# Transposing Q and K by DMA instead of by TensorE, in a block-sparse attention and MLP-mixer kernel

## The chip, the cores and the metric

The kernel runs on one core of a Trainium2 chip. The metric is device time in microseconds (us), the median of several executions; each experiment was timed against the kernel before on the same chip. A run counts as slow when it is over 1.5% above the fastest of its kernel; slow runs are left out of ratios, and where only a slow run was profiled, the text says so. A profile is one execution taken by the hardware profiler; its span is some 1.7 to 2.1 us shorter than the device time. Engines are called as the profile calls them: PE (TensorE matmul), PEld (its weight load), DVE (VectorE), ACT (ScalarE), POOL (GpSimd) and SP (SyncE, which here only issues DMAs).

## The reference

Four batches, eight heads, 768 positions, head width 64. Attention is masked by 32-wide blocks: neighbours, first and last blocks, and three sampled blocks a row. A token mixer and a channel mixer follow.

```python
scores = scale * np.matmul(q, k.transpose(0, 1, 3, 2))
scores = np.where(mask, scores, -1000000000.0)
attn = softmax(scores)
x = np.matmul(attn, v)                         # per head, then heads side by side: 768 x 512 per batch
h = np.maximum(x.T @ w_tok1, 0.0) @ w_tok2     # token mixing
u = x + h.T
out = u + np.maximum(u @ w_ch1, 0.0) @ w_ch2   # channel mixing
```

## The kernel before

The 32 heads go in 16 pairs. Each pair's K and Q arrive as bf16 with positions on partitions; the score matmul is given them with the 64 head columns on partitions. 24 further partitions (64 to 87) of the same tiles hold block indicators and mask rows, so one 88-row matmul gives the masked score.

```python
raw = sbw.tile([128, 2, NC, D], BF16, tag=f"{nm}raw", bufs=NR, ...)   # NR = 4; loaded by POOL, fp32 -> bf16
...
lay = sbw.tile([128, NC, 2, D], BF16, tag=f"{nm}lay", bufs=2, ...)
nc.vector.tensor_copy(out=lay, in_=raw.rearrange("p h c d -> p c h d"))
...
for c in range(NC):                                     # NC = 6, on PE, into PSUM
    nc.tensor.matmul(out=box["t"][:, c, :], lhsT=lays[nm][:, c, :, :], rhs=ident, is_transpose=True)
for hd in range(2):                                     # evacuated by DVE or ACT
    nc.vector.tensor_copy(out=buf[0:64, :], in_=box["t"][64 * hd : 64 * hd + 64, :, :])
...
nc.tensor.matmul(out=ps[:, hd, 0:384], lhsT=ktb[n][0:88, 128 * j : 128 * j + 128],
                 rhs=qtb[n][0:88, 384 * half : 384 * half + 384], start=True, stop=True)
nc.scalar.activation(out=et, in_=ps[:, :, 0:384], func=AF.Exp, scale=0.125)      # 192 of these
```

The order of instructions is made at build time. A small planner simulates PE, ACT and DVE with estimated durations and emits whatever is ready first, by priority: scores, then PV (attention times V), transposes, token mixing, and last channel mixing, which fills what PE time is left. In the traces each engine runs its list **in order**, and an instruction waits for its data whatever the planned durations are.

The softmax here doesn't subtract the row's maximum and nothing guards it: scores larger than these inputs give would overflow.

Of the kernel before, what the change touches and what calls it, by code (L numbers as in the profile page):

```python
# [8 lines left out]
FP32 = mybir.dt.float32  # L9
BF16 = mybir.dt.bfloat16  # L10
# [40 lines left out]
class Planner:  # L51
# [11 lines left out]
    def __init__(self, slots):  # L63
        self.now = 0.0
        self.free_at = {"pe": 0.0, "act": 0.0, "dve": 0.0}
        self.streams = []
        self.ops = []
        self.count = 0
        self.slots = {tag: [Ev(0.0)] * n for tag, n in slots.items()}
        self.exp_pending = 0  # L70
# [32 lines left out]
    def step(self):  # L103
# [3 lines left out]
        if self.free_at["pe"] <= self.now:  # L107
            for s in self.streams:
# [4 lines left out]
                cost, deps, tags, emit, done = s[3]  # L113
# [15 lines left out]
        else:  # L129
            nxt.append(self.free_at["pe"])  # L130
        for eng in ("act", "dve"):
            if self.free_at[eng] > self.now:
# [37 lines left out]
def kernel(  # L170
# [21 lines left out]
    NR = 4  # L192
    NET = 8

    sb1 = ctx.enter_context(tc.tile_pool(name="sb1", bufs=1))
# [12 lines left out]
    vaug = [sb1.tile([128, 2, NC, 66], BF16, name=f"vaug{n}") for n in range(NV)]  # L208
    qtb = [sb1.tile([128, S], BF16, name=f"qtb{n}") for n in range(2 * NV)]
    ktb = [sb1.tile([128, S], BF16, name=f"ktb{n}") for n in range(2 * NV)]  # L210

    P = Planner({"ps": 2, "po": 1, "pm": 3, "et": NET, "a_t": 2, "o": 3, "rc": 2,
                 "lay": 2, "kq": NV, "va": NV})
    US = 1e3
# [110 lines left out]

    rows_there = {("k", n): Ev() for n in range(2 * NV)} | {("q", n): Ev() for n in range(2 * NV)}

    def mask_stream():
# [15 lines left out]
        for h in range(2):  # L344
            def copy(eng, h=h):
                nc.scalar.copy(out=qtb[0][R, 384 * h : 384 * h + 384], in_=pms[h][R, 0:384])
            e2.append(P.op(("act",), {"act": 420.0}, [done], copy, prio=0))
            rels[h].same_as = e2[h]
        rows_there["q", 0].same_as = e2[1]
        for n in range(2 * NV):  # L350
            for nm, bufs in (("k", ktb), ("q", qtb)):
                if (nm, n) == ("q", 0):
                    continue

                def copy(eng, n=n, nm=nm, bufs=bufs):
                    nc.vector.tensor_copy(
                        out=bufs[n][R, :], in_=indf if nm == "k" else qtb[0][R, :]
                    )
                rows_there[nm, n].same_as = P.op(
                    ("dve",), {"dve": 300.0}, e2, copy, prio=2 if n < 2 else 6  # L360
                )
# [4 lines left out]

    ones_there = [Ev() for _ in range(NV)]

    START = 6.5 * US
# [13 lines left out]
    def relayout(p):  # L383
        lays = {}
        for nm in ("k", "q", "v"):
            raw = raws.pop((nm, p))
            arr = arrive.pop((nm, p))

            def emit(eng, nm=nm, raw=raw):
                if nm == "v":  # L390
                    nc.vector.tensor_copy(out=vaug[p % NV][:, :, :, 0:64], in_=raw[:, :, :, :])  # L391
                    return
                lay = sbw.tile([128, NC, 2, D], BF16, tag=f"{nm}lay", bufs=2, name=f"{nm}lay{p}")
                nc.vector.tensor_copy(  # L394
                    out=lay[:, :, :, :], in_=raw[:, :, :, :].rearrange("p h c d -> p c h d")
                )
                lays[nm] = lay

            deps = [arr]
            if nm == "v" and p >= NV:  # L400
                deps.append(pv_done[p - NV])
            if nm != "v" and p >= 2:
                deps.append(qT_there[p - 2, 1])
            lays[nm + "ev"] = P.op(("dve",), {"dve": 320.0}, deps, emit, prio=2 if nm != "v" else 3)
            copied[nm, p] = lays[nm + "ev"]
        va_there[p] = lays["vev"]
        return lays

    def transposes(p):
        for hd in range(2):  # L410
            kT_there[p, hd], qT_there[p, hd] = Ev(), Ev()
        yield lambda: ("v", p) in raws
        lays = relayout(p)
        for nm, bufs, there in (("k", ktb, kT_there), ("q", qtb, qT_there)):
            box, last, rel = {}, Ev(), Ev()
            for c in range(NC):
                def emit(nm=nm, c=c, box=box, rel=rel):
# [7 lines left out]
                    )  # L425
                deps = [lays[nm + "ev"]]
                if p >= NV:
                    deps.append(qk_done[p - NV])
                yield 56.0, deps, [("pm", 1)] if c == 0 else [], emit, last if c == NC - 1 else None
            n_left = [2]  # L430
            for hd in range(2):
                buf = bufs[2 * (p % NV) + hd]

                def evac(eng, hd=hd, buf=buf, box=box):
                    i = box["t"][64 * hd : 64 * hd + 64, :, :].rearrange("p c s -> p (c s)")
                    if eng == "act":
                        nc.scalar.copy(out=buf[0:64, :], in_=i)
                    else:
                        nc.vector.tensor_copy(out=buf[0:64, :], in_=i)  # L439

# [5 lines left out]
    def alias(a, b):  # L446
        a.same_as = b
# [9 lines left out]
    def qk_stream():  # L457
        for s in steps:
# [4 lines left out]
            def emit(s=s, done=done, rel=rel):  # L463
# [4 lines left out]
                for hd in range(2):  # L468
                    n = 2 * (p % NV) + hd
                    nc.tensor.matmul(  # L470
                        out=ps[:, hd, 0:384], lhsT=ktb[n][0:88, 128 * j : 128 * j + 128],
                        rhs=qtb[n][0:88, 384 * half : 384 * half + 384], start=True, stop=True,
                    )
                P.exp_pending += 1

                def exp(eng):
# [12 lines left out]
                326.0,  # L489
                [e for hd in range(2) for e in (  # L490
                    kT_there[p, hd], qT_there[p, hd],
                    rows_there["k", 2 * (p % NV) + hd], rows_there["q", 2 * (p % NV) + hd],
                )],
# [74 lines left out]
    def tok(b, g):  # L568
# [16 lines left out]
        if b not in st:  # L585
            st[b] = dict(u=xs[b], uT_there=[Ev() for _ in range(4)])
        a_rel = Ev()
# [33 lines left out]
        for dmc in (2 * g, 2 * g + 1):  # L621
            last, rel, tbox = Ev(), Ev(), {}
            for sc in range(NC):
                def emit(sc=sc, dmc=dmc, rel=rel, tbox=tbox):
                    if sc == 0:
                        P.take("pm", rel)
                        tbox["pt"] = psM.tile([128, NC, 128], BF16, tag="pm", name=f"pm_ut_{b}_{dmc}")
# [3 lines left out]
                    )  # L631
                yield 56.0, [u_evs[sc // 2]], [("pm", 1)] if sc == 0 else [], emit, last if sc == NC - 1 else None

            def evac(eng, dmc=dmc, tbox=tbox):
                if "uT" not in st[b]:
                    st[b]["uT"] = sbw.tile([128, 4, S], BF16, tag="uT", bufs=B, name=f"uT{b}")
                o, i = st[b]["uT"][:, dmc, :], tbox["pt"][:, :, :].rearrange("p c s -> p (c s)")
# [9 lines left out]
    def ch(b, pool, tag):  # L647
# [4 lines left out]
        for cc in range(12):  # L652
            for sh in range(2):
# [23 lines left out]
                alias(rel, ev)  # L677
                rc_there[cc, sh] = ev
        for sc in range(NC):
            last, rel, pbox = Ev(), Ev(), {}  # L680
# [51 lines left out]
    P.stream(4, ch_stream())  # L732
    P.stream(-1, mask_stream())
    tok2_op = P.op(("dve",), {"dve": 900.0}, [tok2_raw], wtok2_lay, prio=3)

# [56 lines left out]
```

## Time and profile before

| | before |
|---|---|
| device time | 288.56 us (288.53 to 288.65) |
| PE busy | 269.9 us, 94% |
| last exp ends (attention over) | 160.9 us |
| channel matmuls before that | 44 |
| longest gap between exps | 3.0 us, at 32 us |
| DMA engines full until | about 62 us |

The page gives each engine's busy time and then the span in 40 slices, one digit each. The lines that carry the argument are in the prediction below. The last exp's end comes from the ACT timeline.

### The profile page before, as it was taken

The numbers are of one execution on the slowest core, as the hardware profiler recorded it, in microseconds if no ns is written. First come the engines' busy times: TensorE is split into PE (matmuls) and PEld (weight loads), VectorE is DVE, ScalarE is ACT, GpSimd is POOL, SyncE is SP. The second block draws the span as 40 slices with busy tenths as digits, with TensorE's granted clock in tenths as the row PEclk, the third lists the DMA queues.
The fourth block names the chain that finished last, engine by engine and source line by source line (L and its number), as shares of the span: only waits on it lengthen the run. The fifth ranks groups of instructions, "written<-read, shape, count | busy, mean of one in ns | idle before, by whom it ended". The sixth has DMA issues, their size and how long they took to land.

```text
span 287.1 us, 6351 instructions
## 1 busy us (share of the span) xinstructions
PE 269.9 (94%) x2682; PEld 175.5 (61%) x2690; DVE 130.2 (45%) x286; ACT 191.9 (67%) x286; POOL 45.0 (16%) x70
## 2 busy tenths in 40 slices
PE   0799899999999999999999999999999999999994
PEld 0366676678777777777777754456544654456441
DVE  5789966557777569765546341210022001200121
ACT  1589999999999999999999642037501770067200
POOL 7956554522211000000000000000000000000000
PEclk9999999999999999999999999999999999999999
DMA  4999999996254100000000001220022001210122
GB/s 55 134 204 202 214 201 205 201 185 87 39 73 66 23 2 2 0 2 3 2 0 2 2 0 39 106 76 0 2 110 84 29 0 73 94 54 0 38 102 82
DMA packets 19168, 20.07 MB, mean 70 GB/s; under 512 B 1348, under 2 KB 15428, under 8 KB 19140
## 3 DMA queue, kind: packets, MB, share of 16 engines
q0 software_dynamic: 15648, 13.37, 30.3%
q1 hardware_dynamic: 3492, 6.29, 5.8%
q8 instruction: 21, 0.34, 0.5%
q14 instruction: 7, 0.06, 0.1%
HBM read 26.74 MB, written 6.29 MB: 115 GB/s over the span
## 4 chain that ended last, share of the span: by engine, by line
PE 73%; ACT 14%; DVE 6%; issue 2%; DMA 2%; POOL 2%; POOLq 0%; DVEq 0%; ACTq 0%
PE pm_ch L686 22%; PE pm_ch L664 21%; ACT et L478 14%; PE ps L470 14%; PE po L520 8%; PE pm_tok L578 3%; PE pm_tok L603 2%; DMA kraw<-in_k_dram 2%; DVE qtb L439 1%; PE pm_ut L628 1%; PE tq L421 1%; DVE ktb L439 1%; PE tk L421 1%; DVE x L535 1%; DVE klay L394 1%
## 5 line engine op out<-in xcount | busy, mean ns | idle before, releaser
L478 ACT ACTIVATE et<-ps 128x768 bf16<-128x768 f32 x192 | 143.2, 810 | 4.2 <-PE ps L470 3.2
L470 PE MATMUL ps<-qtb,ktb 88*128 88x384 bf16 x384 | 95.3, 329 | 4.0 <-ACT et L478 1.7
L560 ACT ACTIVATE rc<-pm_ch 128x384 bf16<-128x384 f32 x84 | 41.2, 491 | 60.7 <-PE pm_ch L664 44.8
L520 PEld LDWEIGHTS <-et 128*128 128x128 bf16 x1152 | 56.0, 97 | 22.8 <-DVE x L535 1.9
L664 PE MATMUL pm_ch<-uT,w_ch 128*128 128x384 bf16 x384 | 68.6, 326 | 0.2 <-DVE rc L562 0.2
L686 PE MATMUL pm_ch<-w_ch,rc 128*128 128x512 bf16 x280 | 62.4, 379 | 0.4
L520 PE MATMUL po<-vaug,et 128*128 128x65 bf16 x1152 | 61.5, 193 | 0.5 <-ACT et L478 0.2
L694 DVE TENSOR_TENSOR o<-pm_ch,x 128x512 f32<-128x512 f32 x24 | 16.6, 692 | 98.7 <-PE pm_ch L686 98.7
L664 PEld LDWEIGHTS <-w_ch 128*128 128x128 bf16 x384 | 37.0, 98 | 23.1 <-issue 0.3
L686 PEld LDWEIGHTS <-rc 128*128 128x128 bf16 x288 | 28.2, 98 | 33.6
L470 PEld LDWEIGHTS <-ktb 88*128 88x128 bf16 x384 | 34.2, 99 | 11.9 <-issue 4.4
L439 DVE COPY ktb<-tk 64x768 bf16<-64x768 bf16 x29 | 16.0, 552 | 17.5 <-PE tk L421 17.2
L611 DVE TENSOR_TENSOR x<-pm_tok,x 128x512 bf16<-128x512 f32 x24 | 16.2, 687 | 6.8 <-PE pm_tok L603 6.5
L535 DVE TENSOR_TENSOR x<-po,recip 128x384 bf16<-128x384 f32 x32 | 17.8, 557 | 1.1
L439 DVE COPY qtb<-tq 64x768 bf16<-64x768 bf16 x30 | 16.6, 552 | 2.1 <-PE tq L421 1.1
L603 PE MATMUL pm_tok<-a_t,w_tok 128*128 128x256 bf16 x96 | 17.0, 272 | 0.0
L230 POOL DMA_DIRECT2D vraw<-in_v_dram x16 | 12.3, 766 | 28.4 <-DVE vaug L391 25.7
L578 PE MATMUL pm_tok<-x,w_tok 128*128 128x256 bf16 x96 | 16.3, 272 | 0.0
L230 POOL DMA_DIRECT2D kraw<-in_k_dram x16 | 11.6, 727 | 7.7 <-DVE recip L534 2.2
L230 POOL DMA_DIRECT2D qraw<-in_q_dram x16 | 11.5, 720 | 6.4 <-DMA w_ch<-in_moe_w_ch_dram 2.4
L534 DVE RECIPROCAL recip<-po 128x6 f32<-128x6 f32 x32 | 6.2, 195 | 12.0 <-PE po L520 11.6
L421 PE MATMUL tq<-ident,qlay 128*128 128x128 bf16 x96 | 11.3, 230 | 0.2 <-DVE qlay L394 0.2
(49 smaller groups left out, 122.8 us busy)
## 6 DMA issues: line engine op xcount, KB each, us to landing
out_dram<-o SPq DMA_DIRECT2D x24, 256.0 KB, 2.0
kraw<-in_k_dram POOLq DMA_DIRECT2D x16, 192.0 KB, 7.9
qraw<-in_q_dram POOLq DMA_DIRECT2D x16, 192.0 KB, 7.4
vraw<-in_v_dram POOLq DMA_DIRECT2D x16, 192.0 KB, 7.0
w_ch<-in_moe_w_ch_dram POOLq DMA_DIRECT2D x8, 384.0 KB, 9.8
w_tok<-in_moe_w_tok_dram POOLq DMA_DIRECT2D x1, 384.0 KB, 7.8
w_tok2r<-in_moe_w_tok_dram POOLq DMA_DIRECT2D x1, 384.0 KB, 9.0
samp<-in_sampled_blocks_dram SPq DMA_DIRECT2D x1, 0.6 KB
```

Source lines behind the costliest of these rows:

```text
L230: nc.gpsimd.dma_start(out=raw[:, :, :, :], in_=APx(src, 2 * p * S * D, [[NC * D, 128], [S * D, 2], [1, NC * D]]),)
L421: nc.tensor.matmul(out=box["t"][:, c, :], lhsT=lays[nm][:, c, :, :].rearrange("p h d -> p (h d)"), rhs=ident[:, :], start=(c == 0), stop=( ...
L439: nc.vector.tensor_copy(out=buf[0:64, :], in_=i)
L470: nc.tensor.matmul(out=ps[:, hd, 0:384], lhsT=ktb[n][0:88, 128 * j : 128 * j + 128], rhs=qtb[n][0:88, 384 * half : 384 * half + 384], star ...
L478: nc.scalar.activation(out=et[:, :, :], in_=ps[:, :, 0:384], func=AF.Exp, scale=0.125)
L520: nc.tensor.matmul(out=po[:, hd, c, :], lhsT=et[:, hd, 128 * c : 128 * c + 128], rhs=va[:, hd, j, 0:65], start=(j == 0 and hd == 0 and c = ...
L535: nc.vector.tensor_tensor(out=free(xs[b][:, 3 * half, 128 * pb : 128 * pb + 128], 0, [[64, 2], [DM, 3], [1, 64]]), in0=po[:, :, :, 0:64], ...
L560: nc.scalar.activation(out=o(), in_=i, func=AF.Relu)
L578: nc.tensor.matmul(out=box["pm"][:, t, :], lhsT=w_tok1[:, sc, 128 * t : 128 * t + 128], rhs=xs[b][:, sc, 256 * g : 256 * g + 256], start=( ...
L603: nc.tensor.matmul(out=ubox["pm"][:, i, :], lhsT=w_tok2[:, t, 2 * s2 + i, :], rhs=a_t[:, t, :], start=(i == 0 and t == 0), stop=(i == 1 an ...
L664: nc.tensor.matmul(out=pbox["pm"][:, 0:384], lhsT=w_ch1[:, dmc, 128 * cc : 128 * cc + 128], rhs=st[b]["uT"][:, dmc, 384 * sh : 384 * sh + ...
L686: nc.tensor.matmul(out=pbox["pm"][:, :], lhsT=box["rc"][:, cc, 128 * sc : 128 * sc + 128], rhs=w_ch2[:, cc, :], start=(cc == 0), stop=(cc ...
```

## The change

The aim is to take the transposes off PE, and their evacuations off DVE and ACT. From the third pair on, DVE copies raw K and Q into a *wide* tile of 128 columns per head: 64 data columns and 24 mask columns, which were put there once. A DMA transpose (`dma_start_transpose`, in the code and below called the crossbar) writes the whole wide tile, transposed, straight into the operand of the score matmul. These pairs need no PSUM tile and no evacuation: 12 transposes of K and 12 of Q are left on PE, of 96 each. The queue of SP issues the transfers, two for each pair, 393 KB each.

```diff
+    NPE = 2          # pairs 0 and 1 stay with PE
+    NL = 3           # wide buffers for each of K and Q
-    qtb = [sb1.tile([128, S], BF16, name=f"qtb{n}") for n in range(2 * NV)]
+    qtb = [sb1.tile([128, 2, S], BF16, name=f"qtb{n}") for n in range(NV)]
+    wide = {(nm, n): sb1.tile([128, 2, NC, 128], BF16, name=f"{nm}wide{n}")
+            for n in range(NL) for nm in ("k", "q")}
...  # wide_stream: 12 small matmuls, 6 clears and 6 copies put the mask columns into the wide tiles, once
+                elif p >= NPE:
+                    nc.vector.tensor_copy(out=wide[nm, p % NL][:, :, :, 0:64], in_=raw[:, :, :, :])
...
+    def crossbar(p):
+        lays = relayout(p)
+        for nm, bufs, there in (("k", ktb, kT_there), ("q", qtb, qT_there)):
+            def emit(eng, nm=nm, bufs=bufs):
+                nc.sync.dma_start_transpose(
+                    out=bufs[p % NV][:, :, :].rearrange("e h (c s) -> e (h c) s", c=NC),
+                    in_=wide[nm, p % NL][:, :, :, :].rearrange("p h c e -> p (h c e)"),
+                )
...
+            ev = P.op(("sp",), {"sp": 1500.0}, deps, emit, prio=1, lat=2500.0)   # planned: 1.5 + 2.5 us
+            xb_done[nm, p] = ev
+            there[p, 0], there[p, 1] = ev, ev
...
-                    st[b]["uT"] = sbw.tile([128, 4, S], BF16, tag="uT", bufs=B, name=f"uT{b}")
+                            st[b]["uT"] = sbw.tile([128, 4, S], BF16, tag="uT", bufs=3, name=f"uT{b}")
```

More of the change, by code (lines that the diff above doesn't have):

```diff
@@ L64, in __init__ @@
         self.now = 0.0
-        self.free_at = {"pe": 0.0, "act": 0.0, "dve": 0.0}
+        self.free_at = {"pe": 0.0, "act": 0.0, "dve": 0.0, "sp": 0.0}
         self.streams = []
@@ L130, in step @@
             nxt.append(self.free_at["pe"])
-        for eng in ("act", "dve"):
+        for eng in ("act", "dve", "sp"):
             if self.free_at[eng] > self.now:
@@ L208 @@
     vaug = [sb1.tile([128, 2, NC, 66], BF16, name=f"vaug{n}") for n in range(NV)]
-    qtb = [sb1.tile([128, S], BF16, name=f"qtb{n}") for n in range(2 * NV)]
-    ktb = [sb1.tile([128, S], BF16, name=f"ktb{n}") for n in range(2 * NV)]
+    qtb = [sb1.tile([128, 2, S], BF16, name=f"qtb{n}") for n in range(NV)]
+    ktb = [sb1.tile([128, 2, S], BF16, name=f"ktb{n}") for n in range(NV)]
+    wide = {
+        (nm, n): sb1.tile([128, 2, NC, 128], BF16, name=f"{nm}wide{n}")
+        for n in range(NL) for nm in ("k", "q")
+    }
     P = Planner({"ps": 2, "po": 1, "pm": 3, "et": NET, "a_t": 2, "o": 3, "rc": 2,
-                 "lay": 2, "kq": NV, "va": NV})
+                 "uT": 3})
     US = 1e3
@@ L324 @@
     indf = ind[R, :, :].rearrange("k c p -> k (c p)")
-    rows_there = {("k", n): Ev() for n in range(2 * NV)} | {("q", n): Ev() for n in range(2 * NV)}
+    rows_there = {(nm, n): Ev() for nm in ("k", "q") for n in range(2 * NPE)}
+    wide_there = {(nm, n): Ev() for nm in ("k", "q") for n in range(NL)}
     def mask_stream():
@@ L345, in copy @@
             def copy(eng, h=h):
-                nc.scalar.copy(out=qtb[0][R, 384 * h : 384 * h + 384], in_=pms[h][R, 0:384])
+                nc.scalar.copy(
+                    out=qtb[0][R, 0, 384 * h : 384 * h + 384], in_=pms[h][R, 0:384]
+                )
             e2.append(P.op(("act",), {"act": 420.0}, [done], copy, prio=0))
@@ L349, in mask_stream @@
         rows_there["q", 0].same_as = e2[1]
-        for n in range(2 * NV):
+        for n in range(2 * NPE):
             for nm, bufs in (("k", ktb), ("q", qtb)):
@@ L356, in copy @@
                     nc.vector.tensor_copy(
-                        out=bufs[n][R, :], in_=indf if nm == "k" else qtb[0][R, :]
+                        out=bufs[n // 2][R, n % 2, :], in_=indf if nm == "k" else qtb[0][R, 0, :]
                     )
@@ L367, with wide_stream, emit, clear @@
     ones_there = [Ev() for _ in range(NV)]
+    def wide_stream():
+        box, done, rel = {}, Ev(), Ev()
+        def emit():
+            P.take("pm", rel)
+            box["m"] = psM.tile([128, 2, NC, 24], FP32, tag="pm", name="pm_wide")
+            for i, rhs in enumerate((ident[R, 64:88], t2add[R, :])):
+                for c in range(NC):
+                    nc.tensor.matmul(
+                        out=box["m"][:, i, c, :], lhsT=ind[R, c, :], rhs=rhs,
+                        start=(i == 0 and c == 0), stop=(i == 1 and c == NC - 1),
+                    )
+        yield 500.0, [Ev(12.5 * US)], [("pm", 1)], emit, done
+        for n in range(NL):
+            for i, nm in enumerate(("k", "q")):
+                def clear(eng, nm=nm, n=n):
+                    nc.vector.memset(wide[nm, n][:, :, :, 64:128], 0.0)
+                def copy(eng, nm=nm, n=n, i=i):
+                    nc.vector.tensor_copy(
+                        out=wide[nm, n][:, :, :, 64:88],
+                        in_=free(box["m"][:, i, 0, :], 0, [[0, 2], [24, NC], [1, 24]]),
+                    )
+                ev = P.op(("dve",), {"dve": 420.0}, [], clear, prio=6)
+                ev = P.op(("dve",), {"dve": 450.0}, [done, ev], copy, prio=6)
+                wide_there[nm, n].same_as = ev
+                rel.same_as = ev
     START = 6.5 * US
@@ L391, in emit @@
                     nc.vector.tensor_copy(out=vaug[p % NV][:, :, :, 0:64], in_=raw[:, :, :, :])
-                    return
-                lay = sbw.tile([128, NC, 2, D], BF16, tag=f"{nm}lay", bufs=2, name=f"{nm}lay{p}")
-                nc.vector.tensor_copy(
-                    out=lay[:, :, :, :], in_=raw[:, :, :, :].rearrange("p h c d -> p c h d")
-                )
-                lays[nm] = lay
+                elif p >= NPE:
+                    nc.vector.tensor_copy(out=wide[nm, p % NL][:, :, :, 0:64], in_=raw[:, :, :, :])
+                else:
+                    lay = sbw.tile([128, NC, 2, D], BF16, tag=f"{nm}lay", bufs=1, name=f"{nm}lay{p}")
+                    nc.vector.tensor_copy(
+                        out=lay[:, :, :, :], in_=raw[:, :, :, :].rearrange("p h c d -> p c h d")
+                    )
+                    lays[nm] = lay
             deps = [arr]
@@ L401, in relayout @@
                 deps.append(pv_done[p - NV])
-            if nm != "v" and p >= 2:
-                deps.append(qT_there[p - 2, 1])
+            if nm != "v" and 1 <= p < NPE:
+                deps.append(qT_there[p - 1, 1])
+            if nm != "v" and p >= NPE:
+                deps.append(wide_there[nm, p % NL])
+                if p - NL >= NPE:
+                    deps.append(xb_done[nm, p - NL])
             lays[nm + "ev"] = P.op(("dve",), {"dve": 320.0}, deps, emit, prio=2 if nm != "v" else 3)
@@ L407, in relayout @@
         return lays
+    xb_done = {}
+    def crossbar(p):
[5 more added lines that the diff above has]
+                    in_=wide[nm, p % NL][:, :, :, :].rearrange("p h c e -> p (h c e)"),
+                )
+            deps = [lays[nm + "ev"]]
+            if p >= NV:
+                deps.append(qk_done[p - NV])
+            ev = P.op(("sp",), {"sp": 1500.0}, deps, emit, prio=1, lat=2500.0)
+            xb_done[nm, p] = ev
+            there[p, 0], there[p, 1] = ev, ev
     def transposes(p):
+        yield lambda: ("v", p) in raws
+        if p >= NPE:
+            crossbar(p)
+            return
         for hd in range(2):
             kT_there[p, hd], qT_there[p, hd] = Ev(), Ev()
-        yield lambda: ("v", p) in raws
         lays = relayout(p)
@@ L425, in emit, with evac @@
                     )
-                deps = [lays[nm + "ev"]]
-                if p >= NV:
-                    deps.append(qk_done[p - NV])
-                yield 56.0, deps, [("pm", 1)] if c == 0 else [], emit, last if c == NC - 1 else None
-            n_left = [2]
+                yield 56.0, [lays[nm + "ev"]], [("pm", 1)] if c == 0 else [], emit, last if c == NC - 1 else None
             for hd in range(2):
-                buf = bufs[2 * (p % NV) + hd]
-                def evac(eng, hd=hd, buf=buf, box=box):
+                def evac(eng, hd=hd, buf=bufs[p % NV], box=box):
                     i = box["t"][64 * hd : 64 * hd + 64, :, :].rearrange("p c s -> p (c s)")
                     if eng == "act":
-                        nc.scalar.copy(out=buf[0:64, :], in_=i)
+                        nc.scalar.copy(out=buf[0:64, hd, :], in_=i)
                     else:
-                        nc.vector.tensor_copy(out=buf[0:64, :], in_=i)
+                        nc.vector.tensor_copy(out=buf[0:64, hd, :], in_=i)
                 ev = P.op(("dve", "act"), {"dve": 550.0, "act": 740.0}, [last], evac, prio=2)
@@ L468, in emit @@
                 for hd in range(2):
-                    n = 2 * (p % NV) + hd
+                    n = p % NV
                     nc.tensor.matmul(
-                        out=ps[:, hd, 0:384], lhsT=ktb[n][0:88, 128 * j : 128 * j + 128],
-                        rhs=qtb[n][0:88, 384 * half : 384 * half + 384], start=True, stop=True,
+                        out=ps[:, hd, 0:384], lhsT=ktb[n][0:88, hd, 128 * j : 128 * j + 128],
+                        rhs=qtb[n][0:88, hd, 384 * half : 384 * half + 384],
+                        start=True, stop=True,
                     )
@@ L489, in qk_stream @@
                 326.0,
-                [e for hd in range(2) for e in (
-                    kT_there[p, hd], qT_there[p, hd],
-                    rows_there["k", 2 * (p % NV) + hd], rows_there["q", 2 * (p % NV) + hd],
+                [e for hd in range(2) for e in [kT_there[p, hd], qT_there[p, hd]] + (
+                    [rows_there["k", 2 * p + hd], rows_there["q", 2 * p + hd]] if p < NPE else []
                 )],
@@ L585, in tok @@
         if b not in st:
-            st[b] = dict(u=xs[b], uT_there=[Ev() for _ in range(4)])
+            st[b] = dict(u=xs[b], uT_there=[Ev() for _ in range(4)], uT_rel=Ev())
         a_rel = Ev()
@@ L625, in emit @@
                     if sc == 0:
+                        if dmc == 0:
+                            P.take("uT", st[b]["uT_rel"])
+                            st[b]["uT"] = sbw.tile([128, 4, S], BF16, tag="uT", bufs=3, name=f"uT{b}")
                         P.take("pm", rel)
@@ L631, in emit @@
                     )
-                yield 56.0, [u_evs[sc // 2]], [("pm", 1)] if sc == 0 else [], emit, last if sc == NC - 1 else None
+                tags = [("pm", 1)] if sc == 0 else []
+                if sc == 0 and dmc == 0:
+                    tags.append(("uT", 1))
+                yield 56.0, [u_evs[sc // 2]], tags, emit, last if sc == NC - 1 else None
             def evac(eng, dmc=dmc, tbox=tbox):
-                if "uT" not in st[b]:
-                    st[b]["uT"] = sbw.tile([128, 4, S], BF16, tag="uT", bufs=B, name=f"uT{b}")
                 o, i = st[b]["uT"][:, dmc, :], tbox["pt"][:, :, :].rearrange("p c s -> p (c s)")
@@ L678, in ch @@
                 rc_there[cc, sh] = ev
+        alias(st[b]["uT_rel"], last)
         for sc in range(NC):
@@ L733 @@
     P.stream(-1, mask_stream())
+    P.stream(-1, wide_stream())
     tok2_op = P.op(("dve",), {"dve": 900.0}, [tok2_raw], wtok2_lay, prio=3)
```

## The prediction

> **What bounds the kernel now.** I read the busy table and the row of slices first. Columns: engine, busy time, share of the span, instructions; then one digit per fortieth of the span (7.2 us).
>
> ```profile
> PE 269.9 (94%) x2682; PEld 175.5 (61%) x2690; DVE 130.2 (45%) x286; ACT 191.9 (67%) x286; POOL 45.0 (16%) x70
> ...
> PE   0799899999999999999999999999999999999994
> ...
> ACT  1589999999999999999999642037501770067200
> ...
> DMA  4999999996254100000000001220022001210122
> ```
>
> TensorE is full from about slice 7 to the end. ScalarE is full in the first 22 slices (to about 161 us): attention, 192 exps. After that only the channel MLP is left. The DMA engines are full until about 62 us (the loads run ahead of need) and nearly idle afterwards.
>
> A busy PE is not yet a PE that cannot take more, so I counted its work by spacing between starts. The chain of waits, ordered by time, gives the spacings (start, length, what, count):
>
> ```profile
> 144.07 0.39 PE pm_ut L628 x7
> ...
> 189.61 15.60 PE pm_ch L664 x96
> ...
> 205.48 10.74 PE pm_ch L686 x49
> ```
>
> A 128x128 transpose every 56 ns (0.39/7), a 384-column matmul every 162.5 ns, a 512-column one every 219 ns. By the same scaling a 65-column PV matmul takes about 29 ns (groups of 6 stand 0.18 us apart), a 256-column one 109 ns. The busy table by stretch (length, then busy and count of PE, PEld, DVE, ACT, POOL, then clock and DMA):
>
> ```profile
> 12.00:36.00 24.00, 21.86 (x267) 15.18 (x266) 22.26 (x54) 21.29 (x29) 14.40 (x20) 1.00 1.20 201
> 36.00:60.00 24.00, 23.08 (x321) 17.05 (x320) 13.58 (x33) 23.90 (x33) 13.09 (x18) 1.00 1.28 202
> 60.00:161.00 101.00, 100.70 (x1419) 76.98 (x1418) 66.33 (x144) 100.33 (x135) 7.16 (x10) 1.00 0.21 30
> 161.00:288.00 127.00, 121.09 (x664) 64.49 (x670) 20.82 (x32) 42.64 (x86) 0.00 (x0) 0.99 0.13 50
> ```
>
> With counts per source line: in 60 to 161 us PE does 271 QK x 163 = 44.2, 814 PV x 29.3 = 23.9, 133 token matmuls x 109 = 14.5, 72 output transposes x 56 = 4.0, 96 Q/K transposes x 56 = 5.4 and 44 channel matmuls = 7.2: 99.2 of 101 us. So **from 60 us on, PE really is full**: what attention leaves free is filled with channel work of batch 0. In 36 to 60 us the same sum is 21.4 of 24, and in 12 to 36 us about 18 of 24: there the fill does not exist yet, because batch 0 has not been through attention (channel matmuls: 2 before 60 us). The early part is set by ACT and DVE. ACT, as a timeline:
>
> ```profile
> 16.88 15.16 ACT L478 ACTIVATE et<-ps 128x768 bf16<-128x768 f32 x20 [0.16 <-PE ps L470]
> 31.96 1.61 ACT L437 COPY ktb<-tk 64x768 bf16<-64x768 bf16 x2
> 33.91 0.80 ACT L437 COPY qtb<-tq 64x768 bf16<-64x768 bf16 x1 [0.33 <-DVE qtb L439]
> 34.99 27.51 ACT L478 ACTIVATE et<-ps 128x768 bf16<-128x768 f32 x37 [0.29 <-PE ps L470]
> ```
>
> Exps come every 27.51/37 = 0.743 us, except for one hole of 3.0 us (31.96 to 34.99), in which ACT evacuates Q/K transposes because DVE (22.26 of 24 busy) is behind.
>
> [...]
>
> **The change part by part.**
>
> 1. Removed from PE: 14 pairs x 2 x 6 = 168 transposes x 56 ns = 9.4 us. Per-stretch counts of the transposes: 72 before 36 us, 24 in 36 to 60, 96 after 60. Minus 24 that stay (pairs 0 and 1), 72 removed ones lie before 60 us, where PE has holes, and save nothing directly. The **96 after 60 us save 96 x 56 = 5.4 us** on the bounding engine, since channel work moves into the freed time.
> 2. Removed from DVE and ACT: 56 evacuations of 64x768, at 552 ns on DVE (59 there in all) or 795 on ACT (5). About 28 us of DVE and 2.4 us of ACT go. The ACT hole at 32 us should vanish; of its 3.0 us I count **2 us**, since batch 0 then finishes attention earlier and the full stretch of PE begins earlier.
> 3. Added to PE: 12 matmuls of 24 columns for the padded tiles[...].
> 4. Added to DVE: 6 clears of 128x768 and 6 PSUM copies of 288 elements. From the rows for 512 (692 ns) and 384 elements (551 ns), a copy of 288 is about 445 ns; a clear I put at 400 to 700 ns (a 24x768 memset took 698). Together 5 to 7 us. Against it 15 - 7 = 8 mask-row copies x 0.36 = 2.9 us go. The relayout copies (370 ns) stay as copies into the wide tiles. In 12 to 36 us DVE should come out lighter: four pairs of evacuations (4 x 4 x 0.55 = 8.8 us) leave.
> 5. Added to SP and DMA: 28 crossbar transposes of 128x1536 bf16, 393 KB each (twice the useful bytes, because of the padding), 11 MB against the 20 MB moved now. No output store leaves before 177 us, so SP is free for them.
> 6. The buffers of uT go from 4 to 3: token work of batch 3 waits until channel-1 of batch 0 is through. That is 96 x 162.5 = 15.6 us of fill, which before did half of by 161 us (46 matmuls) and the changed kernel about 7.2 + 5.4 = 12.6 us or more. The wait falls in the last token group, where other channel work can stand in: about 0.
>
> Sum if the crossbar keeps up: 5.4 + 2 - 0.6 = 6.8 us, 288.56 - 6.8 = 281.8 us, 2.3% less; with the whole hole won and all of ACT's early losses, some 279; with no early gain 283.5.
>
> **Rivals.**
>
> (a) **The crossbar becomes the bound.** Pair 2's exps begin at about 32 us (24 exps done at 16.88 + 15.16), pair p's at 32 + 8.92 (p - 2), since a pair is 12 x 0.743 = 8.92 us; pair 15's at 148. Pair 2's K is laid out at 17.5 us now, so the first transfer can start at about 20. The 28 transfers have 128 us, less some 2 us for landing (output stores land in 2.0): 4.5 us each is the most that hides. [...]5 or 6 us is not excluded, and each microsecond over 4.5 costs about 28 us at the end of attention, of which PE's channel work hides little, because the order on PE is fixed at build time (the schedule assumes 1.5 us plus 2.5 latency). At 6 us: about 288 + 30 = 320.
>
> (b) **Contention early.** Until 62 us the loads keep the DMA engines full. The first four to eight transposes share them and may take twice as long; pair 2 has 12 us for two, pair 3 has 21 for four. For it: the 1.2 in the DMA column. Against it: the loads run 8 pairs ahead and can give way. Cost if it bites: one to five microseconds of ACT and PE standing still near 32 us, so 283 to 287: within 2%.
>
> (c) **Hidden anyway.** If PE had slack after 60 us, nothing would come of the transposes. The count of 99.2 of 101 speaks against it. If only ACT bound (the chain shows ACT alone from 99 to 126 us), attention would still end at about 158 to 161, and the gain would appear as channel matmuls done before then; it is in the sum.
>
> **How range and chances follow.** I give the crossbar two chances in three to keep up. Then 279 to 284, faster by over 2% (below 282.8) in some 63%: 0.42. Contention or a smaller early gain leaves it within 2% (282.8 to 294.3): 0.25. Crossbar slower than about 4.7 us: 0.33. The middle of all this is a little above the clean sum: 282.5. The range leaves a tenth above 306, for a crossbar well over 5 us.
>
> **What would show it.** Right: no ACT copies after the second pair, exps at 0.743 us without a hole near 32 us, attention ending at 157 to 161 us with 75 or more channel matmuls before it (46 now), PE full to the end, transposes landing within about 4 us. Wrong: PE waiting at the QK matmuls for a DMA into ktb or qtb, exps spaced by transfers and not by 0.743, SP's queue never empty, DMA busy through 150 us; or early DVE time going up with the clears, with pair 2 late. I am most wrong if one 128x1536 transpose takes over 4.5 us.

The sum came to 5.4 + 2 - 0.6 = 6.8 us, so 288.56 - 6.8 = 281.8 us; in the changed kernel the twelve keep PE busy for 0.49 us.

## The result, and the profile after

The changed kernel takes **316.37 us** (median of 4, 315.43 to 317.63), against 288.54 for the kernel before in the same rounds. The ratio is 1.097, with a 95% interval of 1.092 to 1.102. Here and below a ratio is the mean time of one kernel's fast runs over the mean of the other's of the same rounds, so it is not quite the ratio of the medians quoted. The prediction (about 282.5, with a range that ends at 306) was wrong.

The busy table and the slices of the changed kernel (one digit per fortieth of the span, here 7.84 us):

```profile
PE 265.4 (85%) x2525; PEld 169.6 (54%) x2534; DVE 109.4 (35%) x247; ACT 185.6 (59%) x273; POOL 44.9 (14%) x70
...
PE   0798200059999999999999999999999999999995
...
ACT  1589100029999999999999999212750274027400
...
PEclk9999755558999999999999999999999999999999
DMA  3999999999999999555550000022002200220022
```

There is one hole, in slices 5 to 9, in which PE and ACT do nothing, while the DMA row stays at 9. PEclk, the clock granted to PE in tenths, falls to 5 there. The ACT timeline puts the hole between 32.65 and 67.20 us (in brackets, what ended the idle time):

```profile
67.20 1.51 ACT L539 ACTIVATE et<-ps 128x768 bf16<-128x768 f32 x2 [34.55 <-PE ps L530]
...
72.55 123.47 ACT L539 ACTIVATE et<-ps 128x768 bf16<-128x768 f32 x164 [0.58 <-PE ps L530]
```

From 72.55 us on the kernel is as full as before, and an exp takes 123.47/164 = 0.753 us, as before (132 in 99.22 us, 0.752). The queue of SP, as a timeline (start, length, line, what), shows what happened there:

```profile
24.02 7.93 SPq L461 DMA_TRANSPOSE ktb<-kwide  x1
32.01 11.07 SPq L461 DMA_TRANSPOSE qtb<-qwide  x1
43.13 17.23 SPq L461 DMA_TRANSPOSE ktb<-kwide  x2
60.41 5.47 SPq L461 DMA_TRANSPOSE qtb<-qwide  x2
...
158.91 1.43 SPq L461 DMA_TRANSPOSE ktb<-kwide  x1
160.44 1.75 SPq L461 DMA_TRANSPOSE qtb<-qwide  x1
```

The same instruction takes 1.4 to 1.9 us late in the kernel and 8 to 11 us at the start. This length is how long the instruction holds SP's queue, not how long the data move: for the last two transposes the busy table by stretch shows the DMA engines at work from 160.1 to about 163.85 us, 786 KB in 3.75 us, some 210 GB/s or 1.9 us for each. As a sign that the DMA engines are held up it serves all the same, and below it is called the time on SP. From issue to landing, late transposes take 3.8 to 4.2 us; the first two, K and Q, took 20.3 and 21.2. The order of issue shows a second thing: the first two are K and Q of pair **3**. Pair 2 comes third (K) and fifth (Q), because pair p uses wide buffer p mod 3 and buffer 2 got its mask columns last. DVE and PE, as timelines (what ended the idle time is in brackets):

```profile
63.50 0.36 DVE L432 COPY kwide<-kraw 128x768 bf16<-128x768 bf16 x1 [33.64 <-DMA ktb<-kwide]
...
64.00 0.56 DVE L595 TENSOR_TENSOR x<-po,recip 128x384 bf16<-128x384 f32 x1
```

```profile
64.61 0.37 PE L638 MATMUL pm_tok<-x,w_tok 128*128 128x256 bf16 x1 [31.22 <-DVE x L595]
66.31 1.44 PE L530 MATMUL ps<-qtb,ktb 88*128 88x384 bf16 x4 [1.33 <-DMA qtb<-qwide]
```

DVE stood 33.6 us at a copy into a wide buffer that the crossbar had still to read. A norm of pair 1 stood behind that copy, and a token matmul on PE behind the norm. Then PE waited 1.3 us more for Q of pair 2 itself. So two things end within 3 us of each other: DVE's stand at 63.5, and the arrival of Q at 66.3.

The sum in parts. The last exp ends at 196.0 us instead of 160.9, 35.1 later. Of these, 31.6 are the hole (34.6 in place of 3.0), 0.6 its later start, and 2.9 come after it. Most of the 2.9 lie before 72.55 us, where four exps take 5.35 us and the granted clock (the column before the last two) is still 0.51:

```profile
66.30:72.55 6.25, 6.24 (x39) 3.87 (x40) 1.02 (x2) 3.13 (x4) 1.43 (x2) 0.51 1.31 180
```

From the last exp to the end of the span the kernel needs 117.6 us instead of 126.2, 8.6 less: 96 channel matmuls are done before the last exp instead of 44, and 52 x 162.5 ns is 8.5 us. This is the gain that was meant; why it is more than the 5.4 us predicted was not separated. 35.1 less 8.6 is 26.5 us, the difference of the spans (313.6 and 287.1).

### The profile page after: what moved, and what is told of

Its sections match the earlier page's. It is cut to its first block, busy times and chain, and to the rows that moved or that the text cites. A ratio compares the mean times of both kernels' runs of the same rounds, so it can differ in the third digit from the quotient of the medians.

```text
span 313.6 us, 6075 instructions
## 1 busy us (share of the span) xinstructions
PE 265.4 (85%) x2525; PEld 169.6 (54%) x2534; DVE 109.4 (35%) x247; ACT 185.6 (59%) x273; POOL 44.9 (14%) x70
## 3 DMA queue, kind: packets, MB, share of 16 engines
q0 software_dynamic: 15648, 13.37, 28.7%
q1 hardware_dynamic: 47396, 17.31, 27.6%
HBM read 26.74 MB, written 6.29 MB: 105 GB/s over the span
## 4 chain that ended last, share of the span: by engine, by line
PE 78%; DMA 7%; ACT 5%; SPq 4%; DVE 2%; issue 1%; POOL 1%; POOLq 0%; ACTq 0%
PE pm_ch L728 20%; PE pm_ch L751 19%; PE ps L530 19%; PE po L580 10%; DMA ktb<-kwide 6%; ACT et L539 5%; SPq L461 4%; PE pm_tok L638 3%; PE pm_tok L663 3%; DMA qtb<-qwide 2%; PE pm_ut L691 2%; PE tk L487 0%; DVE o L759 0%; DVE eq L320 0%; POOL kraw L236 0%
## 5 line engine op out<-in xcount | busy, mean ns | idle before, releaser
L539 ACT ACTIVATE et<-ps 128x768 bf16<-128x768 f32 x192 | 143.8, 809 | 41.3 <-PE ps L530 40.6
L530 PE MATMUL ps<-qtb,ktb 88*128 88x384 bf16 x384 | 98.3, 339 | 5.0 <-ACT qtb L497 1.6
L728 PE MATMUL pm_ch<-uT,w_ch 128*128 128x384 bf16 x384 | 72.3, 326 | 0.0
L580 PEld LDWEIGHTS <-et 128*128 128x128 bf16 x1152 | 57.7, 99 | 23.6 <-issue 2.7
L620 ACT ACTIVATE rc<-pm_ch 128x384 bf16<-128x384 f32 x73 | 35.8, 491 | 54.9 <-PE pm_ch L728 39.0
L751 PE MATMUL pm_ch<-w_ch,rc 128*128 128x512 bf16 x279 | 62.8, 379 | 0.6 <-DVE o L759 0.2
L580 PE MATMUL po<-vaug,et 128*128 128x65 bf16 x1152 | 62.7, 195 | 0.4 <-ACT et L539 0.3
L530 PEld LDWEIGHTS <-ktb 88*128 88x128 bf16 x384 | 36.1, 100 | 49.3 <-issue 38.7
L759 DVE TENSOR_TENSOR o<-pm_ch,x 128x512 f32<-128x512 f32 x24 | 16.6, 691 | 89.7 <-PE pm_ch L751 89.7
L638 PE MATMUL pm_tok<-x,w_tok 128*128 128x256 bf16 x96 | 17.1, 285 | 31.2 <-DVE x L595 31.2
L432 DVE COPY kwide<-kraw 128x768 bf16<-128x768 bf16 x14 | 5.2, 379 | 35.4 <-DMA ktb<-kwide 35.3
L236 POOL DMA_DIRECT2D vraw<-in_v_dram x16 | 11.5, 721 | 40.3 <-DVE vaug L430 30.3
L622 DVE TENSOR_SCALAR rc<-pm_ch 128x384 bf16<-128x384 f32 x23 | 12.7, 554 | 11.2 <-PE pm_ch L728 11.1
L705 DVE COPY uT<-pm_ut 128x768 bf16<-128x768 bf16 x14 | 7.8, 557 | 4.9 <-PE pm_ut L691 4.9
```

Of the source, the lines that this page charges most:

```text
L236: nc.gpsimd.dma_start(out=raw[:, :, :, :], in_=APx(src, 2 * p * S * D, [[NC * D, 128], [S * D, 2], [1, NC * D]]),)
L530: nc.tensor.matmul(out=ps[:, hd, 0:384], lhsT=ktb[n][0:88, hd, 128 * j : 128 * j + 128], rhs=qtb[n][0:88, hd, 384 * half : 384 * half + 38 ...
L539: nc.scalar.activation(out=et[:, :, :], in_=ps[:, :, 0:384], func=AF.Exp, scale=0.125)
L580: nc.tensor.matmul(out=po[:, hd, c, :], lhsT=et[:, hd, 128 * c : 128 * c + 128], rhs=va[:, hd, j, 0:65], start=(j == 0 and hd == 0 and c = ...
L620: nc.scalar.activation(out=o(), in_=i, func=AF.Relu)
L638: nc.tensor.matmul(out=box["pm"][:, t, :], lhsT=w_tok1[:, sc, 128 * t : 128 * t + 128], rhs=xs[b][:, sc, 256 * g : 256 * g + 256], start=( ...
```

## The experiments

**The theory:** the loads, which fill the DMA engines until about 60 us, slow the transposes that run beside them. The rivals: the first transposes are slow of themselves; or the static order (pair 3 before pair 2, DVE's copy ahead of the norm) makes the hole.

### e1: the same order, few bytes loaded

```diff
+            if p < NR:    # full load; from pair 4 on only 16 of 384 elements a row
-                in_=APx(src, 2 * p * S * D, [[NC * D, 128], [S * D, 2], [1, NC * D]]),
+                in_=APx(src, 2 * p * S * D, [[NC * D, 128], [S * D, 2], [1, 16]]),
...  # w_ch1, w_ch2: memset by POOL instead of loaded; raw tiles kept, so that all is initialised
```

> Same instruction order as the changed kernel, but the loads of pairs 4 to 15 move 16 elements a row instead of 384 and the channel weights are set by memset (wrong result on purpose). Theory (the loads slow the first transposes): the first six transposes take at most 2.5 us each on the SP queue instead of 8 to 11, land within 6 us, ScalarE has no hole over 3 us, device time 276 to 284 us. Rival (the first transposes are slow of themselves, or the order of instructions alone makes the hole): the first six still take 8 us or more or the hole stays over 15 us, device time over 300.

The result is wrong on purpose. The time was 288.87 us, and ACT's waits for scores fell from 40.6 to 13.8 us in all, the longest from 34.6 to 6.2:

```profile
ACT et L542 <- PE ps L533: 13.8, 14, 6.2
```

The first two transposes took 1.49 and 1.85 us on SP instead of 7.93 and 11.07:

```profile
25.33 1.49 SPq L464 DMA_TRANSPOSE ktb<-kwide  x1
26.88 1.85 SPq L464 DMA_TRANSPOSE qtb<-qwide  x1
```

So the loads (the channel weights among them) cause the slowness, and first use does not. The expected time and hole were missed all the same. Two Ks queued together took 3.8 us, two Qs 5.6, and a 6.2 us hole stayed, ended by Q of pair 2, the fifth in line. POOL's queue still has 13,472 of its 15,648 packets, so e1 does not show a quiet DMA.

### e2: pair 2 first; e6: and DVE out of the way

```diff
-    wide[nm, p % NL]
+    wide[nm, (p - NPE) % NL]                                   # e2
-            xb_done[nm, p] = ev
+            xb_done[nm, p].same_as = Later(ev, 18000.0)        # e6 also: a wide buffer counts as free 18 us later
```

> Only the wide buffer of pair p changes, from p mod 3 to (p-2) mod 3, so pair 2 is transposed before pair 3. Theory (contention with loads, plus a static order built on 1.5 us per transpose): the first transposes still take 8 to 11 us each, pair 2's Q lands near 45 to 55 us, the hole shrinks from 34.6 to 13 to 22 us, time 295 to 305. Rival (the order of pairs 3 and 2 is the main cause): hole under 6 us, time under 288.

> As e2 (crossbar from pair 2 on, pair 2 first), with the wide buffer counted free 18 us later. Theory: DVE no longer stands in the way, but pair 2's Q still lands only near 48 us because the loads hold it up; one hole from 32 to about 48 us of 14 to 18 us stays and the later holes of e2 shrink; time 295 to 305. Rival (the order on DVE is all): hole under 5 us and time under 288.

e2 took 310.32 us and had holes of 18.3 and 7.9 us; Q of pair 2, second in line now, alone took 14.68 us on SP. e6 took 313.20 and 306.21 us in its two runs (the profile is of the slower one, which counts as slow, so only its waits are used). In e6 DVE no longer stands at the wide buffers before 72 us, and PE waits for the data itself. The waits of e6 between 30 and 72 us (total, times, longest):

```profile
ACT et L549 <- PE ps L540: 27.5, 7, 19.2
PEld L540 <- issue: 25.9, 4, 19.2
PE ps L540 <- DMA qtb<-qwide: 25.0, 2, 19.1
```

So the order of the pairs is worth 6 us of the 28. What DVE's order is worth here stays open: the one fast run of e6 is 4.1 us below e2, but its two runs lie 7.0 apart. In the changed kernel DVE's stand and the late Q covered the same stretch; removing the first alone leaves the second. The first holes came nearly as expected (18.3 us in e2; 19.2 in e6, for 14 to 18), the times did not: e2 was 5.3 us over the expected 295 to 305, e6's fast run 1.2, because the transposes of pairs 3 and 4 were late too.

### e3, e4: begin later, with pair 6 or pair 8

```diff
-    NPE = 2
+    NPE = 6      # e3; e4: NPE = 8. Buffer order of e2. PE's transposes of pairs 4 and up wait for the last score of pair p - 4
```

> PE transposes pairs 0 to 5 as before, the crossbar takes pairs 6 to 15 (NPE 6, slot order of e2). Theory: the first crossbar transposes still meet the loads and take about 8 to 11 us, but pair 6 is needed only near 68 us, so no hole over 3 us; 120 transposes go from PE, some 100 of them after 60 us; time 279 to 285 us, ratio to before 0.97 to 0.99. Rival (the crossbar costs the engines something else[...]): exps slower than 0.76 us each throughout and time over 288.

> As e3 with the crossbar from pair 8 on. Theory: 96 PE transposes go, nearly all after 60 us, 5.4 us of PE time; no hole; time 280 to 285, at most 2 us slower than e3. Rival as in e3.

Both were slower than before: e3 302.72 us (ratio 1.047), e4 295.91 (1.026). The expectation failed. The rival's sign, slower exps, is absent too: before its hole e4 does 42 exps in 31.37 us, 0.747 us each. The first four transposes of e3 took 4.3, 9.1, 8.1 and 7.8 us; the first two of e4 began at 58.5 us, when 38 of the 48 loads of Q, K and V had been issued, and took 3.8 and 4.7. Pair 8's data were not needed before about 85 us, yet e4 had a hole of 11.3 us at 67 us:

```profile
78.19 0.81 ACT L539 ACTIVATE et<-ps 128x768 bf16<-128x768 f32 x1 [11.30 <-PE ps L530]
```

DVE's waits of e4 between 60 and 120 us name the cause:

```profile
DVE qwide L432 <- DMA qtb<-qwide: 10.5, 3, 5.9
DVE kwide L432 <- DMA ktb<-kwide: 8.5, 4, 5.9
```

The planner had put the copies of pair 11 into pair 8's buffers about 4 us after the transpose's issue. The landings took 10.6 us and 13.0 us. These copies were in no hurry, but norms and PE's next matmuls stood behind them.

### e5, e10: the same, with the reuse planned later

```diff
-            xb_done[nm, p] = ev
+            xb_done[nm, p].same_as = Later(ev, 12000.0)        # e5, NPE = 8;  e10: 22000.0
```

> As e4, but the schedule counts a wide buffer as free only 12 us later than before (16 us after the transpose is issued instead of 4), so DVE's copies into it stand later in its order. Theory (in e4 DVE stood 5.9 us twice at copies into wide buffers that the crossbar still read, and norms and PE stood behind them): the hole of 11.3 us at 67 us goes, waits of DVE for the crossbar under 2 us in all, time 279 to 285. Rival (the crossbar slows the other engines or the data itself is late): a hole over 4 us stays, time over 288.

> As e5 with the wide buffer counted free 22 us later instead of 12. Theory (e5's scatter from 282 to 292 comes from landings that sometimes pass 16 us, behind which DVE's copies stand): all runs 281 to 285, scatter under 3 us. Rival (scatter from late data at QK, or from late loads): scatter as in e5.

e5 ran 281.98, 289.80, 285.66 and 291.80 us; e10 ran 282.01, 281.55, 286.27 and 281.48 (ratio 0.9765, 0.974 to 0.979). In both profiles, which fell on fast runs, DVE has no wait for the crossbar at all, and ACT runs from 36.7 us to the end of attention without a hole. ACT's timeline of e10:

```profile
36.70 123.57 ACT L549 ACTIVATE et<-ps 128x768 bf16<-128x768 f32 x164 [0.27 <-PE ps L540]
```

Nothing but the planned time of a buffer's reuse differs between e4 and e5. So the early place of these copies in DVE's order makes e4's hole. The expected times were missed all the same: three of e5's four runs are over 285 us (its two fast runs average 283.8 us, 0.984 of before), and one of e10's. What goes wrong in these runs no profile caught. Landings of varying length would fit: the longest in e5's fast profile is 15.2 us, just under the planned 16, and in e12 below, with the same plan, DVE waits for the crossbar twice, 5.9 us in all. It is not shown.

### e11: begin with pair 10; e12, e16: fewer loads at once

```diff
+    NPE = 10, reuse 16 us        # e11
+    NPE = 8, reuse 12 us, NR = 3 raw buffers instead of 4, channel weights after pairs 9 and 11 instead of 5 and 7   # e12
+    as e12 with reuse 22 us      # e16
```

> PE transposes pairs 0 to 9, crossbar from pair 10, reuse counted 16 us late. Theory: the loads are through when it starts, 72 PE transposes go, 4.0 us; 283 to 286, scatter under 2 us. Rival (the crossbar costs in any stretch): 288 or more.

> As e5 with three raw buffers instead of four and the channel weights after pairs 9 and 11. Theory: fewer loads meet the transposes in bursts, time 280 to 286; if the weights now come too late for the fill from 60 us, up to 3 us of gain are lost. Rival: scatter as in e5.

> Crossbar from pair 8, reuse counted 22 us late, three raw buffers, channel weights after pairs 9 and 11 (e10 and e12 together). Theory: no hole in any run, 281 to 283 us in all runs, ratio to before 0.975 to 0.98. Rival (e12's small gaps come from its loads arriving late): 282 to 284, no better than e12.

e11: 284.05 us (283.82 to 284.47), ratio 0.985, a gain clear of the noise though under 2%. It removes 72 transposes, 4.0 us at 56 ns, and gains 4.4. e12: 282.45 us (281.84 to 283.19), ratio 0.979, with an interval of 0.977 to 0.982 about the mark of 2%. Both came as expected. **e16: 281.10 us (280.89 to 281.62 in five runs), ratio 0.9738, 95% interval 0.972 to 0.975.** It beats both kernels, its scatter is under 0.8 us, and it is slightly better than expected. Its PE and ACT over 60 to 160 us, from the busy table by stretch (columns as in the prediction):

```profile
60.00:160.00 100.00, 100.00 (x1352) 75.22 (x1350) 53.63 (x119) 99.27 (x132) 12.38 (x17) 1.00 0.77 109
```

84 channel matmuls are through at its last exp (159.7 us), 40 more than before, and 40 x 162.5 ns is 6.5 us; the span is 7.3 us shorter.

### e9: pair 2 with gated loads

```diff
+    NPE = 2, buffer order of e2, reuse 12 us, NR = 2, channel weights after pairs 9 and 11
```

> As e6 (crossbar from pair 2, late reuse, here 12 us), with two raw buffers per operand instead of four, so loads run ahead less, and the channel weights loaded after pairs 9 and 11 instead of 5 and 7. All results correct. Theory (the loads' demand between 20 and 60 us is what slows the first transposes): the first six take 1.5 to 5 us each on SP, the hole at 32 us shrinks from 19 to under 8 us, time 280 to 292. Rival (something else slows them): first six 4 to 16 us as in e6, time over 300.

Two runs, 298.24 and 317.86 us; the profile is of the slower, which counts as slow. The first part came only in part: six transposes of 1.6 to 7.0 us, three of them over the expected 5, and the hole at 32 us broken into pieces of at most 3.4. But the weights now fell beside a later transpose:

```profile
63.31 21.00 SPq L470 DMA_TRANSPOSE qtb<-qwide  x1
```

POOL's timeline has the four loads of w_ch1 issued from 60.6 to 62.8 us. The holes moved to 70 and 86 us (15.0 and 8.0 us). A miss, and a clue: in e2 and e6 too the longest transpose (14.7 and 16.7 us) lay beside w_ch1, whose rows are four times as long as those of Q, K and V.

### e7, e8, e13 to e15: useless loads, by length of row

25 loads of 393 KB, which nobody reads, are put behind the loads of pairs 11 to 15; POOL issues the first at about 56 us. All have the same bytes and differ in their rows of fp32.

```diff
+    nc.gpsimd.dma_start(out=junk[i % len(junk)], in_=APx(q, 0, [[L, 128], [128 * L, 1536 // L], [1, L]]))
     # e7: L = 384, e8: L = 1536, two buffers, on e5
     # e13: L = 384, e14: L = 1536, e15: L = 96, six buffers, on e10; one rc buffer instead of two, to make room
```

> As e5, plus 25 useless loads of 393 KB (fp32 rows of 384 elements, 768 B written each, as Q, K and V have) queued behind the loads of pairs 11 to 15, when otherwise the DMA engines are half idle. Theory (the transposes' 256-byte packets take turns with the loads' packets): transposes that meet them take 6 to 11 us on SP instead of 1.4 to 1.8 as in e5, and land after 12 us or more. Rival (slow only at first use or early in the kernel): they stay under 3 us.

> As e7 with the same bytes in rows of 1536 elements (3072 B written each). Theory (turns by packet, so the time of a transpose grows with the size of the loads' packets): 15 to 40 us for a transpose that lies wholly under these loads. Rival (a fair share of bandwidth by bytes): the same as e7 within 30%.

> As e10 (crossbar from pair 8, reuse 22), plus 25 useless loads of 393 KB after the loads of pairs 11 to 15, into six buffers so that six or more are in flight; one rc buffer instead of two to make room. Rows of 384 fp32 elements (1536 B read). Turns by packet: a transpose has 96 packets of 256 B per DMA engine, each waits for one load packet of 60 to 90 ns, so 7 to 11 us on SP for transposes wholly under the loads. Share by bytes: about the same here.

> As e13 with rows of 1536 elements (6144 B read), the same bytes. Turns by packet: 96 times some 0.24 to 0.37 us, 20 to 36 us for a transpose wholly under the loads. Share by bytes: 7 to 11 us as in e13.

> As e13 with rows of 96 elements (384 B read), the same bytes. Turns by packet: [...]3 to 5 us. Share by bytes: 7 to 11 us as in e13.

The packet times in these expectations are estimates from the profile before: 768 B at 201 GB/s over 16 engines are 61 ns, and 30.3% of 16 engines' 287.1 us over 15,648 packets are 89 ns. e14 has four times these.

e7 (331.13 us): five of the 16 transposes took 6.7 to 7.9 us, two 9.2 and 9.6, the others 1.4 to 5.6. That settles first use: the slowness can be had at 100 us, too. e8 (329.75 us): 1.4 to 11.3 us, no clear difference from e7, so the theory's 15 to 40 us did not come. With two buffers each load waits for the one before last: in e7 POOL stood 51.0 us in ten waits for one of the two. Between 70 and 130 us the rate of the DMA engines falls to 110 GB/s in one slice of e7 and to 80 in one of e8, against 178, 167 and 126 at the lowest in e14, e13 and e15. Whether the queues ran empty was not shown. With six buffers the lengths separate. One line of SP's queue from e13, e14 and e15 each:

```profile
97.94 8.80 SPq L484 DMA_TRANSPOSE qtb<-qwide  x1
```

```profile
98.92 15.87 SPq L484 DMA_TRANSPOSE qtb<-qwide  x1
```

```profile
100.39 5.39 SPq L484 DMA_TRANSPOSE ktb<-kwide  x1
```

| rows of the loads | 384 B (e15) | 1536 B (e13) | 6144 B (e14) | none (late, changed kernel) |
|---|---|---|---|---|
| a transpose under them on SP | 4.9 to 7.0 us (six Ks 2.4 to 3.6) | 7.9 to 9.3 us | 14.4 to 16.6 us | 1.4 to 1.9 us |
| from issue to landing, 80 to 112 us | 10.5 to 16.4 us | 18.3 to 19.1 us | 27.0 to 28.2 us | 3.8 to 4.2 us |

A fair share by bytes would give about one number for all three; that is out. The guess of turns by packet has the right direction: a transpose is 98 packets of some 251 B for each of the 16 DMA engines (the hardware queue has 47,396 packets and 17.31 MB against 3,492 and 6.29 before; the difference over 28 x 16), a useless load is 2,064, 528 or 144 packets for 2,048, 512 or 128 rows, and the more one foreign packet carries, the longer each of the transpose's would wait. Strict turns with a packet time proportional to its row are not borne out: 16 times the row gives about 3 times the time (15.87 against 5.39 us), e14 missed the expected 20 to 36 us, and most transposes of e15 took longer than the expected 3 to 5. How the DMA engines share themselves between loads and transposes is not shown. The times of these kernels (312.20, 314.54, 322.64 us) say nothing by themselves, since their real loads queue behind the useless ones.

## Why the prediction was wrong, point by point

- **PE is the bound from 60 us, and freed PE time fills with channel work: right.** The changed kernel does 52 more channel matmuls before attention ends, 8.5 us; e11 gains 4.4 us for 72 transposes and e16 7.6 us for 96. The clean sum, 281.8 us, is what a kernel without the hole reaches: e10 281.8, e16 281.1. That they agree is in part luck: they take fewer pairs off PE than the change, and what they gain beyond the 5.4 us for 96 transposes was not traced to its parts. An estimate for the full change without a hole is 313.6 - 34.6 = 279.0 us of span, against 279.8 for e16.
- **The early ACT hole of 3.0 us vanishes: not tested cleanly.** In the changed kernel the larger hole covers it; e10 and e16 still use PE there and have no such hole.
- **Rival (a), the crossbar as a steady bound: wrong, though it names a similar time.** Undisturbed, a transpose took 1.9 us of the DMA engines (some 210 GB/s) and landed in about 4.0, so the steady stream stayed hidden, as the clean sum had it. The 320 us given for 6 us each came near 316 by a mechanism that did not occur.
- **Rival (b), contention early: the right mechanism, the term mis-sized. This is the step that failed.** I wrote "may take twice as long", that the loads "can give way", and "one to five microseconds". The first two took 8 to 11 us on SP, five to eight times as long, and 20.3 and 21.2 us to land, five times as long; e1 shows that the loads do it (1.49 and 1.85 us without most of their bytes). The loads did not give way enough, though they ran ahead of need, and the hole was 34.6 us.
- **Two things were left out.** The instruction order put pair 3 before pair 2, so that pair 2's Q waited for four others (worth 6 us, e2). And an order built on 4 us from issue to landing puts DVE's copies where a late landing stops all engines (e4 against e5 and e10). I took the deadline of a transpose to be its score matmul. It is also the next write into its source buffer, and in e4 that one came earlier.
- **DVE's added clears: harmless, as said.** A clear took 378 ns, a PSUM copy 396 to 459, and DVE's busy time fell from 130.2 to 109.4 us. No run isolates uT with three buffers; e10 and e16 have it and reach the sum.
- **Slips of reckoning, without weight.** By the same counts PE's sum for 12 to 36 us is 17.2 us, not about 18; without the early gain the sum gives 283.8, not 283.5; and of the 46 channel matmuls two are counted twice, at the edges of stretches.

## What to carry to other kernels

Before moving work to the DMA engines, look at what else is on them in the very stretch where the first result is due; a mean rate or a mean load over the kernel hides it (before: 70 GB/s on the mean, 201 to 214 between 15 and 57 us). Begin such a change where the loads have run dry, and plan buffers' reuse with the landing time under load, since on an engine that runs its list in order an unhurried copy that waits stops urgent work behind it (33.6 us in the changed kernel). Long rows in bulk loads held up the transposes more than short rows of the same bytes (14.4 to 16.6 us against 4.9 to 7.0 here).
